# Constant matmuls between the score rows of a tuned attention-and-state-space training step, and its skip terms moved to another stage

## Chip, cores, metric

One core of a Trainium2 chip. The metric is the device time of one execution in microseconds (us); each version ran several times, alternating with the kernel before on the same chip. All runs quoted are of the undisturbed state. A profile is one execution. Engines: PE is TensorE, DVE is VectorE, ACT is ScalarE, SP issues transfers. A *bank* is one of the kernel's buffers of 512 columns in PSUM, the memory that PE writes to; an *eviction* is DVE's reading of an accumulator there. The *granted clock* is the share of its full speed at which PE is let run: 0.5 or 1.0 in every record of the traces before (236 records), or the mean over a stretch.

## The reference

Forward and all gradients of a gated sum of softmax attention (no mask, 32 heads of 18) and a diagonal state-space layer, 2048 tokens of 576 numbers, bfloat16:

```python
x = A_x
g = _sigmoid((x * gate_w).sum(-1, keepdims=True))
a = _A_ref(x, A_wqkv, A_wo)                 # softmax attention, 32 heads
b = _B_ref(x, ...)                          # y = conv(u, K) ; y + u * Dskip
return g * a + (1 - g) * b
# reference(): the output and jax.vjp of it for 12 inputs
```

The term `u * Dskip` is the skip term; with the gate it enters the output as `(1-g) * x * Dskip`, the gate's gradient as a dot product with `grad_out`, and the gradient of x as `(1-g) * grad_out * Dskip`.

## The kernel before

Attention runs as a software pipeline of *half-steps* numbered `G`; 32 of them make a unit (a group of four heads, 512 queries), 32 units in all. Each half-step issues a forward stream (P1: scores for the forward exponentials) and, 37 half-steps behind, a backward one (P3: scores recomputed transposed, P2: the products with dO). Six score rows of 512 columns on a quarter of the PE array, in two rounds `x`, then a *burst* into an accumulator. The four bursts of a cycle are dV, dQ and twice half of dK, all in the one bank `accB`; the forward output has its own, `accO`.

```python
OFF = NST + 5                                        # 32 + 5 half-steps
def accB(name):
    return apsp.tile([P, KB], F32, tag="accB", name=name)
def dv_burst(g, b, kq, half):
    acc = accB("accV")                               # dq_burst, dk_half alike
    ...                                              # eight matmuls, then ev(): DVE adds acc to dvacc
# in half-step G, with G2 = G - OFF:
for x in range(2):
    if r1: rows.append(("P1", ...))                  # ps in tag "S", 4 banks
    if r2: rows.append(("P3", ...)); rows.append(("P2", ...))   # "S"; "dP", 2 banks
if G % 4 == 1 and G2 >= 4:        evs.append(dv_burst(...))
if G % 4 == 2 and G2 >= 5:        evs.append(dq_burst(...))
if G % 4 in (3, 0) and G2 >= 10:  e_ = dk_half(...)
if G % 4 in (3, 0) and G >= 3:    ...                # accO: four matmuls
for (kind, g, b, i, j, ps) in rows:                  # P1, P3: ACT exponential; P2: DVE product ds
    ...
```

After attention come the projections (`ps_dwq`, `ps_a`, `ps_dx`, `ps_dwo`), the state-space stage (which the change does not touch) and a last stage that puts the outputs together, tile by tile of 128 tokens (cut):

```python
for t in range(NT):                                  # last stage, first loop
    scalar_tensor_tensor(b_t, x_tok[:, t, :], 1.0, Dskip_b, mult, mult)
    tensor_tensor(b_t, b_t, y_t, add)
    scalar_tensor_tensor(o0, b_t, omg_t[:, t:t+1], ga_t, mult, add); scalar.copy(o0b, o0)
    scalar_tensor_tensor(junk, b_t, 1.0, go_t, mult, mult, accum_out=bgo[:, t:t+1])
...
for t in range(NT):                                  # second loop, after all of dsg and out_12
    tensor_scalar(gy_t, go_t, omg_t[:, t:t+1], mult); tensor_tensor(o1, gy_t, Dskip_b, mult)
    scalar_tensor_tensor(o1, gate_b, dsg[:, t:t+1], o1, mult, add); tensor_tensor(o1, o1, dxm_t, add)
    tensor_tensor(o1[:, half], o1[:, half], prv, add)            # twice
    scalar.copy(o1b, o1)
```

## Time and profile before

Median 3976.87 us. The table divides the profiled execution at first and last instructions of certain kinds:

| stage | from, to | us before |
|---|---|---|
| start | first instruction to first forward exponential | 241.7 |
| forward alone | to first backward exponential | 40.8 |
| **middle**: both streams | to last forward exponential | 2185.0 |
| **tail**: backward alone | to last backward exponential | 65.4 |
| gap and `ps_dwq` | | 113.4 |
| `ps_a`, `ps_dx`, `ps_dwo` | to last matmul of dwo | 114.5 |
| state space | | 1027.9 |
| **last stage** | to the end | 180.9 |

The lines that bound it stand in the prediction. One view more is needed, the waits of PE in the middle (what it waited for: us in total, times, longest):

```profile
PE ps_P L30 <- DMA VaT_g<-VaT_d: 31.8, 7, 5.5
...
PE accK L30 <- DVE dqa L478: 1.3, 6, 0.2
```

PE hardly ever waits in 2185 us: seven times for a load when the head group changes (the only gaps over 3 us), a few us for DVE and ACT. It is busy (95%), at a clock of 0.61.

### The profile page before, as it was taken

The numbers are of one execution on the slowest core, as the hardware profiler recorded it, in microseconds if no ns is written. First come the engines' busy times: TensorE is split into PE (matmuls) and PEld (weight loads), VectorE is DVE, ScalarE is ACT, GpSimd is POOL, SyncE is SP. The second block draws the span as 40 slices with busy tenths as digits, with TensorE's granted clock in tenths as the row PEclk, the third lists the DMA queues.
The fourth block names the chain that finished last, engine by engine and source line by source line (L and its number), as shares of the span: only waits on it lengthen the run. The fifth ranks groups of instructions, "written<-read, shape, count | busy, mean of one in ns | idle before, by whom it ended". The sixth has DMA issues, their size and how long they took to land. (4 is left out here: it accounts for less than half of the span.)

```text
span 3969.6 us, 64388 instructions
## 1 busy us (share of the span) xinstructions
PE 3044.3 (77%) x24050; PEld 1070.9 (27%) x24050; DVE 2943.6 (74%) x5147; ACT 2878.8 (73%) x5308; POOL 62.9 (2%) x141
## 2 busy tenths in 40 slices
PE   8979999999999999999999999598255444544411
PEld 2312222222222222222222222145133333333310
DVE  5628878878778778878778788521488888888877
ACT  4569999989989989989999998311466666666401
POOL 0000000000000000000000000100000000000000
PEclk9956656656566556666665565599565555555555
DMA  8537787887787887887887887966455655665457
GB/s 196 168 98 129 136 160 131 136 160 130 137 158 132 135 158 133 140 157 132 148 150 127 141 142 127 226 173 140 80 104 108 112 104 104 108 109 99 72 145 175
DMA packets 1858940, 538.18 MB, mean 136 GB/s; under 512 B 1771744, under 2 KB 1837354, under 8 KB 1858627
## 3 DMA queue, kind: packets, MB, share of 16 engines
q1 hardware_dynamic: 1858626, 534.07, 70.5%
q8 instruction: 189, 3.10, 0.3%
q14 instruction: 125, 1.02, 0.1%
HBM read 102.10 MB, written 60.96 MB: 41 GB/s over the span
## 5 line engine op out<-in xcount | busy, mean ns | idle before, releaser
L601 DVE TENSOR_TENSOR ds<-ps_P,PT 128x512 bf16<-128x512 f32 x2048 | 1355.2, 687 | 359.7 <-PE ps_P L30 235.5
L592 ACT ACTIVATE PT<-ps_P 128x512 bf16<-128x512 f32 x2048 | 1303.5, 641 | 146.8 <-PE ps_P L30 134.2
L596 ACT ACTIVATE eb<-ps_P 128x512 bf16<-128x512 f32 x2048 | 1318.8, 646 | 21.3 <-PE ps_P L30 21.2
L30 PE MATMUL ps_P<-dOaT,VaT_g 32*128 32x512 bf16 x2048 | 1072.5, 550 | 40.8 <-DMA VaT_g<-VaT_d 31.8
L30 PE MATMUL ps_P<-KaT_g,QaT_g 32*128 32x512 bf16 x2048 | 1030.5, 541 | 34.6 <-ACT PT L592 6.1
L30 PE MATMUL ps_P<-QaT_g,KaT_g 32*128 32x512 bf16 x2048 | 978.3, 556 | 30.0 <-DMA KaT_g<-KaT_d 6.0
L30 PEld LDWEIGHTS <-KaT_g 32*128 32x128 bf16 x2048 | 145.8, 101 | 672.5 <-issue 655.8
L30 PE MATMUL accO<-PT,Vtok_g 128*32 128x512 bf16 x2048 | 307.9, 585 | 0.0
L30 PEld LDWEIGHTS <-VaT_g 32*128 32x128 bf16 x2048 | 192.2, 96 | 409.2 <-issue 368.6
L30 PE MATMUL accK<-dsT,Qtok_g 128*32 128x256 bf16 x4096 | 293.2, 381 | 10.7 <-DMA Qtok_g<-QaT_d 5.4
L30 PE MATMUL accQ<-ds,Ktok_g 128*32 128x512 bf16 x2048 | 242.6, 568 | 1.3 <-DVE dvacc L461 0.8
L30 PE MATMUL accV<-eb,dOa 128*32 128x512 bf16 x2048 | 242.0, 567 | 0.6 <-DVE dkacc L502 0.6
L30 PEld LDWEIGHTS <-QaT_g 32*128 32x128 bf16 x2048 | 174.0, 98 | 168.5 <-issue 157.0
L30 PE MATMUL uvp<-RX,E1e 128*128 128x64 bf16 x1152 | 134.2, 290 | 106.3 <-DVE E1e L892 106.3
L30 PE MATMUL tps<-RX,T0w 128*128 128x32 bf16 x576 | 38.4, 233 | 215.2 <-DVE yd L1027 189.9
L873 ACT ACTIVATE kk<-ph,magc 128x512 f32<-128x512 f32 x144 | 91.2, 686 | 147.7 <-DVE E1e L891 112.7
L30 PE MATMUL ph<-thr,lrow 3*128 3x512 bf16 x288 | 126.7, 569 | 86.8 <-ACT ab L866 60.1
L461 DVE TENSOR_TENSOR dvacc<-dvacc,accV 128x512 f32<-128x512 f32 x224 | 153.5, 685 | 34.5 <-PE accV L30 31.0
L478 DVE TENSOR_TENSOR dqa<-dqa,accQ 128x512 f32<-128x512 f32 x224 | 153.2, 684 | 26.6 <-PE accQ L30 22.6
L30 PEld LDWEIGHTS <-E1e 128*128 128x128 bf16 x1152 | 125.3, 123 | 127.3 <-DVE E1e L892 126.7
L30 PE MATMUL ybp<-Rw,E1n 128*128 128x31 bf16 x1152 | 70.1, 233 | 103.5 <-ACT ydi L964 100.8
L878 DVE SCALAR_TENSOR_TENSOR kk<-kk,ph 128x512 f32<-128x512 f32 x144 | 95.1, 681 | 73.0 <-ACT kk L873 73.0
(273 smaller groups left out, 3374.9 us busy)
## 6 DMA issues: line engine op xcount, KB each, us to landing
T0w<-Kp_d SPq DMA_DIRECT2D x36, 512.0 KB
dsT<-ds SPq DMA_TRANSPOSE x512
dqkv_d<-dtk SPq DMA_DIRECT2D x96, 72.0 KB
dqkv_tok<-dqkv_d SPq DMA_DIRECT2D x1, 6912.0 KB
Md_d<-mst SPq DMA_DIRECT2D x144, 36.0 KB
ga_d<-ga_st SPq DMA_DIRECT2D x16, 288.0 KB
dxm_d<-dxm SPq DMA_DIRECT2D x16, 288.0 KB
skw<-Md_d SPq DMA_DIRECT2D x72, 64.0 KB
```

What stands on the lines that cost most here:

```text
L30: return nc.tensor.matmul(out, lhsT=lhsT, rhs=rhs, start=start, stop=stop, **kw)
L461: nc.vector.tensor_tensor(a_, a_, acc, op=A.add)
L478: nc.vector.tensor_tensor(U["dqa"], U["dqa"], acc, op=A.add)
L592: nc.scalar.activation(U["PT"][i][:, j, :], ps, ACT.Exp)
L596: nc.scalar.activation(e, ps, ACT.Exp)
L601: nc.vector.tensor_tensor(U["ds"][i][:, j, :], ps, U["PT"][i][:, j, :], op=A.mult)
L873: nc.scalar.activation(B_["kk"][h][:, 4 * q:4 * q + 4, :], ph, ACT.Identity, bias=magc, scale=1.0)
L878: nc.vector.scalar_tensor_tensor(v_, v_, MAGIC, B_["ph"].pop((h, q)), op0=A.subtract, op1=A.subtract)
```

## The change

Its intent: keep the TensorE clock up in attention with matmuls whose result is thrown away, in three of the four half-steps of a cycle, two full-array ones of 512 columns each. They are written into the accumulator that the burst after them overwrites (`start=True`), so they need no bank of their own; for that the accumulator is taken before the second round of rows. The backward stream goes from 37 to 39 half-steps behind. The bursts of dV, dQ and dK are now tied to `G2 % 4`. The skip terms are computed beside the projections, and the last stage has two DVE operations per output tile and one loop in place of two.

```diff
-                OFF = NST + 5
+                OFF = NST + 7
+                ACC = []
+                fill_r = ident_bf.unsqueeze(1).to_broadcast([P, 4, P])
+                def fill(acc, n, w=4):
+                    o_ = acc[:, (4 - w) * P:4 * P].rearrange("p (a b) -> p a b", b=P)
+                    for _ in range(n):
+                        mm(o_, lhsT=J_bf, rhs=fill_r[:, 0:w, :])
-                    acc = accB("accV")                     # also accQ, accK
+                    acc = ACC.pop()
+                    ph = G2 % 4 if 4 <= G2 < NTOT + 4 + (0, 1, 6, 0)[G2 % 4] else None
+                    if ph == 2 and G2 < 10:
+                        ph = None
                     for x in range(2):
+                        if x == 1 and ph in (0, 1, 2):
+                            ACC.append(accB(("accV", "accQ", "accK")[ph]))
+                            fill(ACC[0], NFILL)            # NFILL = 2
-                    if G % 4 == 1 and G2 >= 4:
+                    if G2 % 4 == 0 and G2 >= 4:            # dV
-                    if G % 4 == 2 and G2 >= 5:
+                    if G2 % 4 == 1 and G2 >= 5:            # dQ
-                    if G % 4 in (3, 0) and G2 >= 10:
+                    if G2 % 4 in (2, 3) and G2 >= 10:      # dK
 ...                 (accO unchanged: if G % 4 in (3, 0) and G >= 3)
 ...                 ps_a loop:
-                    nc.vector.tensor_scalar(d_a_tok[:, t, :], go_t, g_t[:, t:t + 1], None, op0=A.mult)
+                    nc.vector.tensor_tensor(xd, x_tok[:, t, :], Dsk_b, op=A.mult)
+                    nc.vector.scalar_tensor_tensor(ga_st, xd, omg_t[:, t:t + 1], ga_st, op0=A.mult, op1=A.add)
+                    nc.vector.scalar_tensor_tensor(xd, xd, 1.0, go_t, op0=A.mult, op1=A.mult, accum_out=bxo[:, t:t + 1])
 ...                 ps_dx loop:
-                    (copy of ps to dxm, on DVE or ACT in turn)
+                    nc.vector.scalar_tensor_tensor(gyd, go_all[:, t, :], omg_t[:, t:t + 1], Dsk_b, op0=A.mult, op1=A.mult)
+                    nc.vector.tensor_scalar(d_a_tok[:, t, :], go_all[:, t, :], g_t[:, t:t + 1], None, op0=A.mult)
+                    nc.vector.tensor_tensor(dxm..., gyd..., ps[:, :, 0:DH2], op=A.add)
 ...                 last stage, per tile (the operations of before are shown above):
+                        nc.vector.scalar_tensor_tensor(o0b, y_t, omg_t[:, t:t + 1], ga_t, op0=A.mult, op1=A.add)
+                        nc.vector.scalar_tensor_tensor(junk, y_t, 1.0, go_t, op0=A.mult, op1=A.mult, accum_out=bgo[:, t:t + 1])
 ...
+                        nc.vector.scalar_tensor_tensor(o1, gate_b, dsg[:, t:t + 1], dxm_t, op0=A.mult, op1=A.add)
+                        nc.vector.tensor_tensor(o1b..., o1..., prv[:, :, 0:DH2], op=A.add)
```

Cut: smaller splits (the follow-up of the output in three pieces instead of two, some double buffers made single) and the parameter gradients, transposed by DMA instead of PE.

## The prediction

It stands here as recorded, with marked cuts: what no trace or run of this case shows is taken out, here and in five of the expectations below.

What it sums per window of 3.41 us is called *use* below: the columns of the matmuls, each times the share of the array that it takes (a quarter for a row of 32 x 128), as a share of the columns that PE can take in that time. At full clock two fills of 512 columns start 0.215 us apart (median of 696 pairs in the kernel after); at half clock half that rate is taken. So the 7168 columns of four half-steps are 3.01 us of their 4 x 1.91 us, a use of 0.39, and the 10,240 with fills 4.30 us, a use of 0.56. Counted again in the middle of before and after, by the starts of the matmuls: the 102 full-clock windows that were followed by half clock had at most 0.39; but so had 78 of the 633 that stayed. The "column-tiled ones" are the matmuls of a burst (1490.94 to 1491.48 in the trace before); that their 0.54 us holds for two fills as well was an estimate.

> **What bounds the kernel now.** I read the page first: the engine sums and the 40 slices. They show three stages in a row.
>
> ```profile
> PE 3044.3 (77%) x24050; PEld 1070.9 (27%) x24050; DVE 2943.6 (74%) x5147; ACT 2878.8 (73%) x5308; POOL 62.9 (2%) x141
> ...
> PE   8979999999999999999999999598255444544411
> PEld 2312222222222222222222222145133333333310
> DVE  5628878878778778878778788521488888888877
> ACT  4569999989989989989999998311466666666401
> ...
> PEclk9956656656566556666665565599565555555555
> ```
>
> Slices 3 to 25 are attention: PE and ACT both near full, but the granted TensorE clock is only 0.5 to 0.6. Then come the projections, the state-space stage (which the change leaves alone), and two last slices with DVE full. Next the groups of instructions, then the table of stretches:
>
> ```profile
> L592 ACT ACTIVATE PT<-ps_P 128x512 bf16<-128x512 f32 x2048 | 1303.5, 641 | 146.8 <-PE ps_P L30 134.2
> L596 ACT ACTIVATE eb<-ps_P 128x512 bf16<-128x512 f32 x2048 | 1318.8, 646 | 21.3 <-PE ps_P L30 21.2
> ```
>
> ```profile
> 282.00:2467.00 2185.00, 2082.11 (x15860) 529.28 (x15859) 1742.39 (x2890) 2040.77 (x4063) 36.93 (x86) 0.61 0.80 141
> 2467.00:2532.00 65.00, 62.51 (x448) 12.21 (x444) 61.90 (x107) 43.67 (x83) 2.58 (x6) 0.53 0.96 165
> ...
> 2647.00:2689.00 42.00, 39.44 (x230) 20.64 (x230) 17.30 (x46) 12.16 (x17) 0.00 (x0) 0.88 0.69 199
> 2689.00:2762.00 73.00, 71.80 (x535) 49.93 (x534) 8.06 (x19) 6.70 (x12) 0.74 (x5) 1.00 0.64 153
> ...
> 3808.00:3901.00 93.00, 7.96 (x34) 3.50 (x35) 92.28 (x175) 14.42 (x31) 0.00 (x0) 0.50 0.56 167
> 3901.00:3970.00 69.00, 14.13 (x110) 5.71 (x109) 48.10 (x98) 10.75 (x16) 0.00 (x0) 0.50 0.72 148
> ```
>
> Columns: stretch, length, busy us of PE, PE weight load, DVE, ACT, Pool, then clock, DMA share, GB/s. Full attention (282 to 2467) holds some 1004 half-steps, so 2185 / 1004 = 2.18 us each. Each half-step has four exponentials; ACT starts them every 0.477 us when it never waits, so **ACT's floor is 4 x 0.477 = 1.91 us**. Sorting the half-steps by the clock records: those wholly at full clock have a median of 1.91 us (ACT-bound), those at half clock a mean of 2.27 us (PE-bound: rows, rows, then a burst of about 1 us). A mean clock of 0.61 says 22% of the time is at full clock. The end of the kernel is DVE-bound: 140 us busy in 162.
>
> [...]every clock record is 0.5 or 1.0 and lasts a multiple of 3.41 us. I summed, per window, matmul columns times the share of the 128x128 array they use. In attention, half-clock windows followed by full clock have a median use of 0.75 of the half-rate cycles (those that stay low 0.68); full-clock windows that fall back have at most 0.38 of the full-rate cycles, those that stay have 0.35 to 0.48.[...] eight column-tiled ones in two waves show 0.54 us from first start to the next rows[...].
>
> **The change, part by part.**
>
> (1) *Fills.* In three of four half-steps two full-array 512-column constant matmuls go into the accumulator before the second rows. Array use per four half-steps, in columns: now rows 4 x 768 plus bursts 4 x 1024 = 7168[...]. With fills 7168 + 3072 = 10,240[...]. So I expect full clock for 80 to 95% of attention, PEclk digits of 9. But a fill must wait until the previous burst's accumulator has been read by DVE[...], so the second rows wait behind it. I work that loop out from a full-clock stretch of the timeline:
>
> ```profile
> 1491.71 0.68 DVE L461 TENSOR_TENSOR dvacc<-dvacc,accV 128x512 f32<-128x512 f32 x1
> ...
> 1495.52 0.39 PE L30 MATMUL ps_P<-dOaT,VaT_g 32*128 32x512 bf16 x1
> ...
> 1495.96 0.69 DVE L601 TENSOR_TENSOR ds<-ps_P,PT 128x512 bf16<-128x512 f32 x1 [0.29 <-PE ps_P L30]
> ```
>
> From one fill to the next: two fills[...] 0.54, to the last row matmul 0.12, row to DVE 0.44 (1495.52 to 1495.96), the ds product's pitch 0.61, the eviction 0.68, the semaphore 0.05 (measured where PE waited for DVE): **2.44 us**, twice. Over the two dK half-steps, which have one fill: fill 0.54, row to ACT 0.41, one exponential's pitch 0.48, the next one's duration 0.60, its bank back to PE 0.06, row to DVE 0.44, ds 0.61, the half-width eviction 0.41, semaphore 0.05: 3.60 us. Sum 2.44 + 2.44 + 3.60 = 8.48 us for four half-steps, **2.12 us each** against ACT's 1.91. So PE's speed is gained and much of it goes into the new wait. With per-unit and group work (about 0.07 us per half-step; some ACT extras fit the slack) 2.19: no gain at all. If ACT sets the pace instead, 1.91 + 0.12 = 2.03, which gains 150 us. My terms lean to the first, but[...] somebody chose two fills, presumably because they paid. I choose a 50 us gain.
>
> (2) *Offset +2 half-steps.* Two more half-steps with only half the work: about +4 us; in the tail (65 us now, DVE-bound) the fill loop may add 5 us. It also leaves more time for the dO transpose, whose wait is now under 2 us. I put -50 + 9 = **-41 us** for attention.
>
> (3) *Skip terms beside the projections.* DVE per ps_a tile goes from 1.2 us (0.76 + 0.37 + 0.08) to about 3.2 us (product 0.75, two fused 0.80 and 0.75, readers 0.16, old product 0.76): 51 us for 16, where the loop took 42. So **+9 us**. In the ps_dx loop DVE gets 0.80 + 0.37 + 0.76 = 1.9 us per tile beside PE's 3.85: hidden.
>
> (4) *Last stage.* DVE loses, by its groups' busy time, 11.6 + 11.8 (skip term into b_t), 5.8 + 12.0 + 12.0 (gate product, skip, dxm), 2.7 + 2.5 (casts and copies of the parameter gradients) and 0.5: 59 us of 140, leaving 81. ACT's two casts per tile go too, and the 15.7 us wait of DVE for o1b, held up behind the tiny out_12 stores, moves: those stores now come last, and their landing (12.9 us waited for now) stands partly at the very end, about +10. DMA has to move 16 x 1.33 = 21 MB in that time; at 240 GB/s (what 3880 to 3900 reached) 88 us, about as long as DVE. I expect 110 us for what takes 162: **-52 us**.
>
> Sum: 3977 - 41 + 9 - 52 = 3893; rounded to **3890 us**.
>
> **Rivals.** (A) *ACT becomes the bound in attention*: for it, full-clock half-steps are exactly 1.91 now and idle PE time is there to fill; against it, the loop above. It gives 3977 - 150 + 9 + 9 - 52 = 3793. (B) *The accumulator wait takes all*: 2.12 and more; only the last stage pays: 3977 + 9 + 9 - 52 = 3943, maybe 3960. (C) *The clock still falls*[...]. (D) *DMA holds attention back*: share 0.80 now, at 1.91 us it would be 0.91; it may delay the dsT transposes in units that load a new group.
>
> **Range and chances.** 2% faster is 3897. A and the point just pass it, B does not. I give A and its neighbourhood 0.3, in between 0.4, B 0.25, C 0.05. Range 3800 to 3960. Faster 0.55, same 0.42, slower 0.03.
>
> **What would show it.** Right: PEclk at 9 through attention; fills waiting for dvacc and dqa of DVE; ACT idle a little for ps_P; half-steps 2.0 to 2.15; the ps_a loop near 50 us; the last stage near 130 us from the state-space end instead of 181, with DVE work near 81. Wrong: PEclk still at 6[...]; attention under 2130 us (the loop has a term too large, A holds); no fill waits for DVE; a last stage still at 150 (DMA-bound).

## The result, and the profile after

**3993.32 us** median (3990.72 to 3995.52) against 3977.36 of the kernel before on the same chip: ratio 1.0036, 95% interval 1.0019 to 1.0053, so "same" by the 2% rule, a little slower in truth, and outside the predicted range. A ratio here is the mean time of one kernel's fast runs over that of the other's of the same rounds, so not quite the ratio of the medians quoted.

| stage | before | after | difference | predicted |
|---|---|---|---|---|
| start | 241.7 | 253.8 | +12.1 | 0 |
| forward alone | 40.8 | 42.7 | +1.9 | +4 (offset) |
| **middle** | 2185.0 | 2179.4 | **-5.6** | -50 |
| **tail** | 65.4 | 106.4 | **+41.0** | +5 |
| gap and `ps_dwq` | 113.4 | 114.4 | +1.0 | 0 |
| `ps_a`, `ps_dx`, `ps_dwo` | 114.5 | 127.0 | +12.5 | +9 |
| state space | 1027.9 | 1029.4 | +1.5 | 0 |
| **last stage** | 180.9 | 136.5 | **-44.4** | -52 |
| sum | 3969.6 | 3989.6 | +20.0 | -84 |

The start is not the change's: all the kernels below have the same code there and show 244.3 to 256.9 us. Its length goes with the clock in it: 0.90 or 0.91 in the profile before and in those of e10 and e15 (241.7 to 245.3 us), 0.85 to 0.88 in all others (249.6 us and more). The middle is not repeated exactly either: the same attention code took 2185.0 us in the profile before and 2174.7 in that of e4, so its -5.6 is no change.

From the page of the kernel after, PE busy and the granted clock in 40 slices; then the table of stretches (columns as in the prediction):

```profile
PE   7978888888888888888888888858445444444421
...
PEclk9959999999989999999999999578655555555555
```

```profile
296.00:2476.00 2180.00, 1875.66 (x17303) 565.24 (x17302) 1733.75 (x2885) 2049.50 (x4057) 36.93 (x86) 0.97 0.70 141
2476.00:2582.00 106.00, 96.03 (x534) 18.69 (x533) 68.08 (x113) 48.77 (x86) 2.58 (x6) 0.53 0.54 111
...
3875.00:3990.00 115.00, 14.54 (x114) 7.21 (x114) 86.13 (x162) 0.00 (x0) 0.00 (x0) 0.50 0.68 201
```

The clock in the middle is 0.97 instead of 0.61, just as wanted, and PE is *less* busy (1876 of 2180 us) and yet nothing is gained. The waits of PE in that stretch say why:

```profile
PE accK L30 <- DVE dqa L490: 75.0, 213, 0.4
PE accQ L30 <- DVE dvacc L473: 69.4, 174, 0.8
PE ps_P L30 <- DMA VaT_g<-VaT_d: 38.3, 7, 6.9
```

Before, the first was 1.3 us and the second did not exist. One turn of the wait, in the timeline (start, duration, engine, line, operation; in brackets the idle time before it and what ended it):

```profile
1504.44 0.59 PE L30 MATMUL accQ<-ident_bf,J_bf 128*128 128x512 bf16 x2 [0.82 <-DVE dvacc L470]
...
1504.97 0.39 PE L30 MATMUL ps_P<-KaT_g,QaT_g 32*128 32x512 bf16 x1
...
1505.39 0.60 ACT L610 ACTIVATE PT<-ps_P 128x512 bf16<-128x512 f32 x1 [0.68 <-PE ps_P L30]
1505.46 0.69 DVE L619 TENSOR_TENSOR ds<-ps_P,PT 128x512 bf16<-128x512 f32 x1 [0.47 <-PE ps_P L30]
...
1506.06 0.68 DVE L490 TENSOR_TENSOR dqa<-dqa,accQ 128x512 f32<-128x512 f32 x1
...
1506.79 0.38 PE L30 MATMUL accK<-ident_bf,J_bf 128*128 128x512 bf16 x1 [0.35 <-DVE dqa L490]
```

Fill to second rows 0.53, rows to the product ds 0.49, ds to the eviction 0.60, eviction to the next fill 0.73: 2.35 us for this half-step. ACT, whose floor is 1.91, idles 0.68 us for the row that stands behind the fill. Over all full-clock cycles the medians of the three legs are 2.35, 2.35 and 3.60 (the last spans two half-steps): 8.30 us for four, **2.075 us each**.

The tail, where only the backward stream is left, in the timeline of PE alone:

```profile
2530.95 1.01 PE L30 MATMUL accQ<-ident_bf,J_bf 128*128 128x512 bf16 x2 [0.31 <-DVE dvacc L473]
2531.89 0.60 PE L30 MATMUL ps_P<-KaT_g,QaT_g 32*128 32x512 bf16 x1
```

The clock is at half, so the pair takes 0.94 us up to the rows.

The last stage: the operation for the output before, and the one before which DVE waited longest; then what is left of its groups after (line, operation, count, busy us and mean ns, idle before):

```profile
L1231 DVE SCALAR_TENSOR_TENSOR o<-b_t,omg_t,ga_t 128x576 f32<-128x576 f32 x16 | 12.9, 806 | 0.0
...
L1269 DVE TENSOR_TENSOR o<-gy_tg,Dskip_b 128x576 f32<-128x576 bf16 x16 | 12.0, 749 | 15.7 <-ACT o1b L1277 15.7
```

```profile
L1270 DVE SCALAR_TENSOR_TENSOR o0b<-y_t,omg_t,ga_t 128x576 bf16<-128x576 bf16 x16 | 12.9, 803 | 3.8 <-DMA ga_t<-ga_d 3.8
L1285 DVE SCALAR_TENSOR_TENSOR o<-gate_b,dsg,dxm_t 128x576 f32<-128x576 f32 x16 | 12.4, 805 | 0.0
...
L1287 DVE TENSOR_TENSOR o1b<-o,prv 128x576 bf16<-128x576 f32 x16 | 11.4, 741 | 0.0
```

The operation of L1269 and the wait of 15.7 us before it are gone; writing bfloat16 directly costs DVE nothing (803 ns against 806 before), so ACT's casts vanish as well.

### The profile page after: what moved, and what is told of

The parts are those of the page before. It is cut to its first block, busy times and chain, and to the rows that moved or that the text cites. A ratio compares the mean times of both kernels' runs of the same rounds, so it can differ in the third digit from the quotient of the medians.

```text
span 3989.6 us, 66887 instructions
## 1 busy us (share of the span) xinstructions
PE 2879.5 (72%) x25556; PEld 1114.0 (28%) x25556; DVE 2941.1 (74%) x5131; ACT 2863.9 (72%) x5253; POOL 63.8 (2%) x147
## 5 line engine op out<-in xcount | busy, mean ns | idle before, releaser
L30 PE MATMUL ps_P<-dOaT,VaT_g 32*128 32x512 bf16 x2048 | 815.5, 400 | 39.2 <-DMA VaT_g<-VaT_d 38.3
L30 PE MATMUL ps_P<-KaT_g,QaT_g 32*128 32x512 bf16 x2048 | 803.2, 396 | 34.9 <-ACT PT L610 6.6
L30 PE MATMUL ps_P<-QaT_g,KaT_g 32*128 32x512 bf16 x2048 | 793.3, 398 | 26.1 <-ACT PT L610 11.7
L30 PEld LDWEIGHTS <-J_bf 128*128 128x128 bf16 x1600 | 151.0, 98 | 473.0 <-issue 413.0
L30 PE MATMUL accQ<-ident_bf,J_bf 128*128 128x512 bf16 x512 | 161.8, 399 | 84.6 <-DVE dvacc L473 73.4
L30 PE MATMUL accK<-ident_bf,J_bf 128*128 128x512 bf16 x512 | 156.2, 387 | 89.0 <-DVE dqa L490 78.2
L30 PE MATMUL accK<-dsT,Qtok_g 128*32 128x256 bf16 x4096 | 210.9, 284 | 10.2 <-DMA Qtok_g<-QaT_d 10.1
L30 PE MATMUL accO<-PT,Vtok_g 128*32 128x512 bf16 x2048 | 213.1, 401 | 0.0
L30 PE MATMUL accV<-ident_bf,J_bf 128*128 128x512 bf16 x512 | 165.2, 406 | 44.0 <-DVE dkacc L514 12.5
L30 PE MATMUL accQ<-ds,Ktok_g 128*32 128x512 bf16 x2048 | 162.7, 396 | 0.0
```

The source lines that it names most:

```text
L30: return nc.tensor.matmul(out, lhsT=lhsT, rhs=rhs, start=start, stop=stop, **kw)
```

## The experiments

Theory T: at full clock the fills make PE wait for the accumulator, and this loop, not ACT, sets the pace; at half clock, in the tail, they simply lengthen PE's work. Rival R1: the fills' own PE time is what costs. Rival R2: another part (the offset, the placing of bursts, the moved skip terms) eats the gain.

Fifteen kernels were run, all correct. Ratios are against the kernel before in the same rounds; the changed kernel is 1.0036. "Middle" and "tail" are from each run's profile. The 95% interval of a ratio is 0.002 to 0.0035 either way, so a difference between two runs of less than some 15 us is not clear of noise.

| run | fills per cycle, where | offset | accO beside | median us | ratio | middle | its clock | tail |
|---|---|---|---|---|---|---|---|---|
| (changed kernel) | 6, accumulator | 39 | dV, dQ | 3993.32 | 1.0036 | 2179 | 0.97 | 106 |
| e1_no_fill | none | 39 | dV, dQ | 3981.65 | 1.0027 | 2215 | 0.70 | 68 |
| e8_no_fill_off5 | none | 37 | dK | 3950.84 | 0.9931 | 2180 | 0.64 | 66 |
| e12_acco_moved | none | 39 | dK | 3926.36 | 0.9861 | 2152 | 0.66 | 67 |
| e3_tail | 6, accumulator, not in the tail | 39 | dV, dQ | 3942.67 | 0.9930 | 2181 | 0.96 | 68 |
| e4_att_before | none (attention of before) | 37 | dK | 3941.61 | 0.9925 | 2175 | 0.63 | 64 |
| e14_change_acco | 6, accumulator | 39 | dK | 3980.45 | 1.0015 | 2174 | 0.96 | 104 |
| e6_fill4 | 12, accumulator | 39 | dV, dQ | 4259.67 | 1.0699 | 2458 | 0.98 | 92 |
| e2_row_bank | 6, row bank | 39 | dV, dQ | 3917.24 | 0.9867 | 2155 | 0.91 | 69 |
| e7_row_all | 8, row bank | 39 | dV, dQ | 3857.03 | 0.9697 | 2084 | 0.97 | 67 |
| e9_row_all_off5 | 8, row bank | 37 | dK | 3888.67 | 0.9767 | 2121 | 0.96 | 64 |
| e10_row_all_one | 4, row bank | 37 | dK | 3873.68 | 0.9733 | 2112 | 0.94 | 64 |
| e11_row_all_one_far | 4, row bank | 39 | dV, dQ | 3881.79 | 0.9740 | 2126 | 0.91 | 67 |
| e13_row_all_vat2 | 4, row bank | 39 | dV, dQ | 3868.67 | 0.9716 | 2101 | 0.92 | 68 |
| e15_row_all_acco | 8, row bank | 39 | dK | 3832.01 | 0.9656 | 2067 | 0.98 | 67 |
| e16_row_all_one_acco | 4, row bank | 39 | dK | 3821.88 | 0.9619 | 2053 | 0.97 | 67 |

### Which part of the change does what: no fills, no fills in the tail, the old attention

```diff
# e1_no_fill
-            NFILL = 2
+            NFILL = 0
# e3_tail
-                            fill(ACC[0], NFILL)
+                            fill(ACC[0], NFILL if G < NTOT else 0)
# e4_att_before: the attention section of the kernel before, all else as changed
```

> The changed kernel with no fills (offset, skip terms and last stage as changed). Theory (the fills trade a slow clock for a wait on the accumulator, and cost the tail): clock 0.6 again in attention, half-steps mean about 2.18 us, middle of attention about as long as before (2185 us), tail 65 to 72 us instead of 106; total 3945 to 3965. Rival (the fills gain in the middle and something else, the offset or the buffers cut to one, eats it): without fills the kernel gets slower than the changed one, over 4010.

Measured 3981.65 us, between the two: neither expectation held. The tail falls from 106 to 68 us as the theory wants, but the middle is *worse* than before the change:

```profile
296.00:2510.00 2214.00, 2077.80 (x15825) 516.82 (x15823) 1763.52 (x2883) 2026.35 (x4052) 36.93 (x86) 0.70 0.68 139
```

So with accO beside dV and dQ the fills gain some 36 us in the middle (2215 to 2179) and lose about 38 in the tail (e14 below shows what that gain is worth); and something else in the change costs 30 to 40 us in the middle. The half-clock half-steps point to it: their medians in the four phases are 2.37, 1.93, 1.91, 2.82 us, where the kernel before has 2.14, 2.31, 2.14, 2.29. With the offset moved by two, dV and dQ fall on the half-steps that carry accO, so PE has two heavy and two light half-steps.

> Fills only while forward rows remain; none in the tail of attention. Theory (tail at half clock, where fills are paid at 0.5 us each): the tail goes from 106 to about 68 us, the rest unchanged, total 3993 - 38 = 3955 (3945 to 3965). Rival (the tail is long because of the later offset or DMA): over 3980.

Measured 3942.67 us, ratio 0.9930, the tail 67.5 us: confirmed (the whole 2 us under the range). Against the changed kernel that is 0.0106 x 3977 = 42 us. In the stretches, its tail has PE at 64 us of 67 instead of 96 of 106:

```profile
296.00:2476.00 2180.00, 1881.89 (x17298) 565.37 (x17295) 1733.34 (x2884) 2047.68 (x4054) 36.93 (x86) 0.96 0.69 141
2476.00:2543.00 67.00, 63.82 (x472) 12.60 (x472) 65.37 (x112) 45.54 (x86) 2.58 (x6) 0.55 0.89 174
```

> Attention of the kernel before; skip terms, projections and last stage as changed. Theory (those parts give -44 + 11 = -33 us): 3977 - 33 = 3944 (3935 to 3955). Rival (the first 12 us that the changed profile lost before attention belong to these parts): 3955 or more.

Measured 3941.61 us, ratio 0.9925: confirmed. Everything but attention gains 30 us (last stage 135 for 181 us, projections 128 for 114); the attention part of the change costs 0.0111 x 3977 = 44 us.

### The placing of accO and the distance

```diff
# e8_no_fill_off5 (NFILL = 0 as well)
-                OFF = NST + 7
+                OFF = NST + 5
# e12_acco_moved (NFILL = 0, OFF = NST + 7)
-                    if G % 4 in (3, 0) and G >= 3:
-                        i_ = (G - 3) // 4 * 2 + (1 if G % 4 == 0 else 0)
+                    if G % 4 in (1, 2) and G >= 2:
+                        i_ = (G - 2) // 4 * 2 + (1 if G % 4 == 1 else 0)
```

> The changed kernel without fills and with the backward stream at its old distance (37 half-steps behind, not 39); everything else of the change stays: the accumulator's bank taken before the second rows, the split of the output's follow-up, the single buffer of dqa, the last stage. Theory: what made the run without fills 30 to 40 us slower in the middle than the kernel before (2215 against 2175 to 2185 us) is where the later stream puts the accO burst: with the dV and dQ bursts instead of the shorter dK ones. With the old distance the middle is 2170 to 2190 us, the half-step medians are again all between 2.1 and 2.35 us, and the whole is that of the run with the old attention, 3930 to 3955 us (ratio 0.990 to 0.996). Rival: the loss comes from one of the other small moves, then the middle stays at 2205 to 2220 and the whole at 3970 to 3990 us.

Measured 3950.84 us, middle 2180: confirmed, as the half-step medians are (2.31, 2.19, 2.17, 2.11).

> The changed kernel without fills, backward stream at the changed distance of 39 half-steps, but the accO burst moved by hand to the two dK half-steps, as the kernel before has it. Theory: what cost the run without fills 35 us was which half-steps carry accO[...], not the distance: middle 2170 to 2195 us, whole 3935 to 3960 us (ratio 0.990 to 0.996), medians of the four half-steps between 2.1 and 2.35 us. Rival: the distance itself costs (more live buffers, later transposes): middle 2205 to 2220, whole 3970 to 3990 us.

Measured 3926.36 us, middle 2152, medians 2.07, 2.31, 2.18, 2.31: the theory is right and the size was too small, 0.0166 x 3977 = 66 us against e1. It is the placing, not the distance, that costs; the longer distance even gains over e8, where PE waits 18.5 us in 14 places for the transposed dO, which e12 does not. In the kernel with its fills this stays hidden:

> The changed kernel as it is, fills in the accumulators, with only the accO burst moved to the two dK half-steps. Theory: at full clock the wait for the accumulators sets the pace (8.30 us per four half-steps) and accO is not in that loop: full-clock legs stay 2.35, 2.35, 3.60, the middle within 20 us of 2179, the tail as before the move, the whole 3970 to 4000 us (ratio 0.998 to 1.006). Rival: the burst beside dV and dQ lengthens the loop: without it the middle falls by 35 us or more as in the runs without fills (2215 to 2152), the whole under 3960.

Measured 3980.45 us, ratio 1.0015, legs again 2.35, 2.35, 3.60, middle 2174: confirmed. In the changed kernel the accumulator loop sets the pace, whatever accO does. And beside e12, the same kernel without fills, the fills now *lose* in the middle too (2152 to 2174), and 61 us in all by the ratios (0.0154 x 3977, of which 37 in the tail): what they seemed to gain against e1 only made good the uneven placing of accO.

### The loop itself: fills in another bank, fills doubled

```diff
# e2_row_bank: the fill goes into the bank of the second round's P1 row, before that row's own matmul
                     ps = apsp.tile([P, KB], F32, tag=tg, bufs=nb, name="ps_" + kind)
+                    fill(ps, nf)           # nf = 2 for the P1 row of x == 1 in phases 0, 1, 2; else 0
-                            fill(ACC[0], NFILL)
# e6_fill4: the changed kernel with NFILL = 4
```

> The changed kernel with four fills instead of two in each accumulator (the suspected cost doubled). Theory: the wait for the accumulator is the loop that sets the pace at full clock; measured in the changed kernel it is 2.35 + 2.35 + 3.60 = 8.30 us per four half-steps. Two more fills of 512 columns add [...]0.43 us to each of its three legs: 9.58 us, 2.40 us per half-step instead of 2.075, over some 980 half-steps +314 us, and about +25 us in the tail: 4310 to 4350 us, ratio 1.08 to 1.095. Rival: PE has slack[...], the fills only use it up, and what costs is something else: within 40 us of the changed kernel's 3993.

Measured 4259.67 us, ratio 1.0699; the legs are 2.78, 2.78 and 4.03, each longer by the 0.43 us of two more fills, exactly as the loop says. The whole is below the expected figures: the middle grows by 279 us for the 314 expected. An undisturbed unit takes 77.8 us for 67.9, which is 9.9 for the 10.2 expected; the units with a change of group, which wait for loads anyway, grow by only 6 to 8. The tail is *shorter* than in the changed kernel:

```profile
299.00:2757.00 2458.00, 2158.39 (x18771) 702.66 (x18770) 1728.28 (x2883) 2105.68 (x4055) 36.93 (x86) 0.98 0.62 125
2757.00:2849.00 92.00, 74.41 (x596) 22.91 (x592) 66.42 (x114) 48.05 (x86) 2.58 (x6) 0.98 0.62 127
```

Four fills keep the clock up in the tail (0.98), two did not (0.53). R1 alone can't explain the doubling: PE still stands idle for 300 us in this middle (2158 of 2458), and waits for DVE at each fill. But the loop contains the fills, so their time counts in full.

> The same fills at the same places in PE's order, but written into the PSUM bank that the next row overwrites, so that no fill waits for DVE's read of the accumulator; none in the tail, where there is no such row. Theory (the wait for the accumulator is what keeps 2.07 us per half-step): clock stays near 1.0 and half-steps fall to ACT's 1.91 plus unit work, about 2.03 with group waits; middle about 2060 to 2090, tail near 70, total 3800 to 3860. Rival[...]: half-steps stay at 2.07, total 3950 or more.

Measured 3917.24 us: the direction right, the gain over the changed kernel (0.0169 x 3977 = 67 us) about half of the least that was expected. And most of it is the tail, which has no fills here (106 to 69). The fair comparison is e3, without fills in the tail too: 0.0063 x 3977 = 25 us, all of it in the middle (2181 to 2155). There the fills are the same in number and place; only the bank differs. The full-clock half-steps fall to medians of 1.91 to 1.94 us, ACT's floor: T confirmed against R1. But the clock does not stay up:

```profile
PEclk9958989989989989989989989588555555555555
```

In the timeline of PE, the fall and the return:

```profile
1504.55 0.37 PE L30 MATMUL ps_P<-KaT_g,QaT_g 32*128 32x512 bf16 x1
...
1505.04 0.99 PE L30 MATMUL ps_P<-ident_bf,J_bf 128*128 128x512 bf16 x2
...
1508.44 0.61 PE L30 MATMUL ps_P<-ident_bf,J_bf 128*128 128x512 bf16 x2
```

At 1505 the fill pair takes 0.99 us, at 1508 again 0.61: one window of 3.41 us at half clock, after two half-steps with dK and almost no other work, of which the second has no fill. The 3.41 us before it hold 12 rows and two halves of dK, 2560 columns, a use of 0.31; by the author's count every full-clock window of this run that was followed by a fall had at most 0.39 (median 0.33). The half-step in this spell takes 3.40 us (1505.04 to 1508.44).

### Fills in all four half-steps

```diff
# e7_row_all: as e2_row_bank, nf = 2 for the P1 row of x == 1 whenever G2 >= 4
# e9_row_all_off5: e7 with OFF = NST + 5;   e10_row_all_one: e9 with NFILL = 1
# e11_row_all_one_far: e7 with NFILL = 1
# e15_row_all_acco, e16_row_all_one_acco: e7 and e11 with accO moved as in e12
# e13_row_all_vat2: e11 with two buffers for VaT_g, some work buffers single
```

> As the run with fills in the banks of the next score rows, but with two fills in all four half-steps of each cycle instead of three (none in the tail). Theory: in that run the full-clock half-steps were already 1.91 to 1.94 us (bound by ACT), and what kept it at 3917 us was that the clock fell about every tenth microsecond beside the half-step without fill. With 4096 instead of 3072 fill columns per cycle [...]no half-step is bare, so the clock stays at 0.97 or more in the middle of attention, the median half-step stays near 1.91, the middle takes 2040 to 2080 us (e2: 2155), and the whole 3805 to 3850 us (ratio 0.958 to 0.970). Rival: the half-steps of dV and dQ, which also have the accO burst, become too long for PE with fills in all[...], so half-steps go to 2.0 and more and the time stays at 3880 to 3920.

Measured 3857.03 us, ratio 0.9697, middle 2084, clock 0.97: at the edge of the expected figures (a few us outside in time), the mechanism confirmed, the rival not. (The expectation has the clock of e2 fall too often: the trace has 99 falls in 2155 us, one in 22 us.) Undisturbed units take 64.1 us, 2.00 per half-step, instead of 67.9 in the changed kernel.

```profile
PEclk9959999999999999999999998599555555555555
```

> The first run of this call (two fills in every half-step, in the bank of the next score row) with the backward stream at its old distance of 37 half-steps. Theory: at full clock ACT sets the pace, so the placing of accO hardly matters now: the same as the first run or up to 20 us faster, with full-clock half-steps at 1.91 us in all four phases. Rival (PE bound in the dV and dQ half-steps even at full clock): over 30 us faster than the first run.

Neither: 3888.67 us, 31 us *slower* than e7. The waits of PE show why:

```profile
PE ps_P L30 <- DMA VaT_g<-VaT_d: 37.6, 7, 6.3
PE ps_P L30 <- DMA dOaT<-dOa: 22.5, 13, 2.8
```

The transpose of dO comes late in 13 units, and the clock falls within 2 us of 11 of these waits. In e7 the second line is absent. The quicker half-steps are not the main reason: e8, which has the same distance and the clock mostly at half, waits as much, and e4, with the old attention at that distance, does not. Here is the line of e8, then that of e4:

```profile
PE ps_P L30 <- DMA dOaT<-dOa: 18.5, 14, 2.7
...
PE ps_P L30 <- DMA dOaT<-dOa: 1.1, 1, 1.1
```

In e8 and e9 the transpose is issued 7.4 and 6.5 us (medians) after ACT's copy of the output, in e4 5.2 us: they have the change's split of the output's follow-up, whose last piece comes a half-step later. No run undid the split alone. The two half-steps more make room for it: e15 below, which differs from e9 in the distance alone, is 0.0111 x 3977 = 44 us faster.

> As the third run of this call, with one fill per half-step instead of two: 2048 columns per cycle[...]. Theory[...]: the clock still stays up over 0.95 and the time is within 15 us of the third run. Rival[...]: mean clock 0.8 to 0.9 and 20 to 80 us slower than the third run.[...]

Measured 3873.68 us, clock 0.94, just under the expected 0.95: faster than e9 by about 0.0034 x 3977 = 14 us, within the 15 expected and not clear of noise. Its use was 0.49 in the median full-clock window.

> Fill in the bank of the next score row in all four half-steps, one instead of two, backward stream at the changed kernel's distance of 39 half-steps. Theory: at full clock ACT sets the pace, one fill is enough to hold the clock (measured with distance 37: clock 0.94 in the middle), and the longer distance hides the transposed dO that the run at distance 37 waited for at nearly every unit (3.9 to 6.4 us): no such waits, the middle 2070 to 2095 us, the whole 3835 to 3865 us (ratio 0.965 to 0.972). Rival: the clock needs two fills at this distance since the dK half-steps carry no accO burst here: clock 0.85 to 0.92, the whole 3880 to 3920.

The rival held: clock 0.91, 3881.79 us. (The waits of e10 for dO were 19, of at most 3.4 us, not as many and as long as the expectation has them.) With accO beside dV and dQ, a dK half-step has 1792 columns with its fill, a dV or dQ one 2816; with accO beside dK all have 2304, and the clock is 0.97 (e16 below).

> As the second run of this call, with two buffers for VaT of the head group instead of one (some small work buffers go from two to one to make room), to see what a version beyond the change reaches. At each of the seven group switches PE now waits some 7 us for the load of VaT, which can't start before the old group's last row, and the clock falls in that wait: a half-step of about 10 us. Theory: seven times about 8 us go, the middle is 50 to 60 us shorter than in the second run: 3780 to 3810 us. Rival: another load of the group (Ktok, Qtok, also single) takes the place of the wait within a few half-steps: under 20 us gained.

The rival held in size, not in cause: 3868.67 us, by the ratios 10 us less than e11, within the noise. The 41.7 us of waits for VaT are gone, but PE then waits 35.0 us, up to 5.3 at a time, for exponentials, and ACT for one of the buffers that this run itself cut to one (e11 has no such wait):

```profile
ACT gb L422 <- DMA gT<-gb: 34.7, 8, 6.3
```

So what a second buffer for VaT is worth stays open.

> Two fills in the bank of the next score row in every half-step, distance 39, and accO moved beside dK. Theory: the run with two fills is bound by ACT already (half-steps 1.91, units of 64.1 us), so the even load changes little: within 15 us of that run's 3857 (ratio 0.966 to 0.973). Rival: PE is at its edge in the dV and dQ half-steps: over 20 us faster.

Measured 3832.01 us, ratio 0.9656: just beyond the lower end, 0.0041 x 3977 = 16 us faster than e7, hardly clear of noise; near the theory.

> One such fill per half-step, distance 39, accO beside dK. Theory: with one fill the clock fell (0.91 in the middle) because windows over the dK half-steps, without accO, had too little use; with accO there every half-step has 768 + 1024 + 512 columns, a use of 0.50, so the clock is 0.95 or more and the whole 3835 to 3865 us (ratio 0.964 to 0.972). Rival: one fill is too little whatever the placing: clock 0.91 and 3870 to 3890 us again.

Measured **3821.88 us**, ratio 0.9619 (0.9597 to 0.9640): 13 us below the range, the clock as expected. The fastest of all, 3.8% faster than the kernel before and 4.2% than the changed one:

```profile
296.00:2347.00 2051.00, 1885.54 (x16804) 628.60 (x16802) 1735.57 (x2884) 1998.63 (x4053) 36.73 (x86) 0.97 0.72 150
```

## Why the prediction was wrong, point by point

The miss is 3993 - 3890 = 103 us. By the stage table: middle 44, tail 36, start 12 (chance), last stage 8, projections 4; the rest cancels. The steps that failed are the choice at the end of part (1) of the prediction (point 2) and the 5 us for the tail in part (2) (point 3).

1. **The clock forecast was right.** "Full clock for 80 to 95% of attention": 0.97 in the mean. The use (0.39 before, 0.56 with fills) pointed the right way, and so it went on: clock 0.91 where one half-step has no fill (e2) or one fill meets an uneven load (e11), 0.97 with two fills everywhere (e7) or one and an even load (e16). That a certain use is needed was inference; no run shows a threshold.
2. **The loop was right, the choice against it was wrong.** The prediction worked out 8.48 us for four half-steps, and wrote "no gain at all". Measured: 8.30. The difference is mostly the 0.12 us for a "last row matmul" (the second rows start together: their bank is free by then). Shown by e6 (each leg +0.43), e2 (the loop removed, half-steps at ACT's floor) and e14 (legs unchanged with accO moved). The failed step is the sentence "somebody chose two fills, presumably because they paid. I choose a 50 us gain." That is no evidence: the middle gained 6. A change's existence says nothing of its worth.

   Yet "no gain at all" came out so well partly by luck, for its slips cancel. The loop is 2.075 us per half-step and not 2.12. The prediction counts 1004 half-steps in the middle; the trace has 1973 forward exponentials there, two to a half-step, so 987, of 2.21 us each and not 2.18. And for unit and group work it allows 0.07 us per half-step. After, 985 half-steps took 2179.4 us, 2.21 each, 0.14 more than the loop's 2.075: 0.05 of it in every undisturbed unit (67.9 us / 32 = 2.12), the rest mostly in the units with a change of group (73.7 to 80.5 us).
3. **"In the tail (65 us now, DVE-bound) the fill loop may add 5 us" was wrong.** It added 41, and e3 takes 42 us off the whole by leaving those fills out. The line printed in the prediction has PE at 62.5 of 65 us there, as full as DVE at 61.9, and the clock at 0.53. So PE had no room for more: with 39 half-steps, some ten cycles of three pairs at 0.94 us are 28 us, and PE's waits for DVE in that stretch add up to 10. The prediction shows no working for its 5; its loop was worked out for the full clock, and here the clock was half.
4. **Not foreseen: the placing of accO.** The offset of two moves the dV and dQ bursts onto the half-steps of accO. Against e1 it costs 38 us (e8, which has the old distance too) to 66 us (e12) without fills, nothing visible with the accumulator fills (e14), and, by the ratios, 16 us (e15 against e7, hardly clear of noise) to 48 us (e16 against e11) once the loop is gone. The prediction priced the offset at "about +4 us" for two half-steps.
5. **The skip terms: right.** "+9 us" for the `ps_a` loop: 36.8 to 45.3 us, with PE waiting for DVE there for 10.8 us instead of 2.6. Beyond it, 4 us appear in `ps_dwo`: before, 31 of its 160 matmuls filled PE's pauses in the `ps_a` loop (the first began at 2649.6, three us after the loop's first); now its operand is made in the `ps_dx` loop, and the whole of 19.9 us comes after that.
6. **The last stage: right in mechanism.** "110 us for what takes 162": 115. DVE's work fell to 86, not 81. And 22 instead of 19 us pass before it starts.
7. **Rival B** ("the accumulator wait takes all; only the last stage pays", 3943 to 3960) was the right story; with the tail's 36 us on top it is 3979 to 3996, and 3993 was measured. It got a chance of 0.25. Its 3960 has no term of its own, so the close fit of the upper end is luck.

## What to carry to other kernels

Work added only to keep a clock up must not wait for anything: put it where its bank is free anyway (here the next score row's), not behind a buffer that another engine has to empty; and spread it evenly: here four fills per cycle gave a clock of 0.97 with the bursts even (e16) and 0.91 with them uneven (e11), and six with one half-step bare no more than 0.91 (e2). Leave it out of stretches that are already bound by the same engine at half clock (the tail: 42 us, e3). Judge it beside the best version without it (here e12), not only beside the one that it came with. When a pipeline offset moves, look at which bursts now share a step, and when the arithmetic of a loop says "no gain", do not overrule it with the thought that the author must have had a reason.

## What the traces showed besides

- Busy is not use. In the kernel before PE was busy 95% of the middle, with gaps over 3 us only at the seven changes of head group, and ran at a clock of 0.61; in e16 it was busy 92% and had 0.97. In the middle of before, the 422 half-clock windows that stayed low and the 77 that were followed by full clock have the same median busy share, 1.00, and a median use of 0.66 and 0.76. The use does not part them sharply either: in before and after together 76 of the 103 half-clock windows that rose had 0.70 or more, but so had 117 of the 438 that stayed low (for full clock see beside the prediction). What sets the clock was not shown.
- Each of the seven waits at a change of head group in the kernel after (3.2 to 6.9 us) has a fall to half clock, 0.3 to 3.3 us after its start.
- At full clock two fills start 0.215 us apart, and the quarter-array rows 0.309 us after the second (medians of 696 pairs): 0.09 us more. What it is was not shown.
- Matmuls added to hold the clock, placed in the accumulator, brought waits for DVE of 75.0 and 69.4 us in two groups and no gain worth the name; in the next row's bank these waits are gone but for 5.3 us (e16), and the full-clock half-steps of e2 are within 0.03 us of ACT's floor.
- The recorded duration of one and the same ACT instruction can grow by half while its pitch stays: in e2 ten exponentials from 1501.19 to 1505.50 start 0.47 to 0.49 us apart and have records of 0.85 to 0.95 us; in the kernel before the pitch is 0.478 and the mean record 0.64. In ten of e16 the pitch is 0.477 and the record 0.71 to 0.83. The pitch of the starts is the cost, not the duration.
